# Attention before a top-1 mixture of experts: router logits issued one round later, their transposes two

## The chip, the cores and the metric

The kernel runs on one core of a Trainium2 chip. The time is the device time of one execution in microseconds (us), as the median of several runs. A profile is one further execution with the hardware profiler on. The engines: TensorE (PE, with its weight loads as PEld), VectorE (DVE), ScalarE (ACT), GpSimd (POOL); SyncE (SP) issues most DMAs. Each engine works through its own queue of instructions in the order in which the program wrote them, and waits on semaphores for the others.

## What is computed

The reference, cut to what matters:

```python
def _attn_ref(q, k, v, n_global, n_local):            # 4 x 8 heads, 768 rows, 64 wide; 8 and 96
    scores = np.matmul(q, k.transpose(0, 1, 3, 2)) / np.sqrt(D)
    keep = is_global | is_local                        # first 8 keys, and the last 96 up to the row's own
    scores = np.where(keep, scores + bias[None], -1e9)
    a = np.exp(scores - scores.max(-1, keepdims=True))
    a = a / (a.sum(-1, keepdims=True) + 1e-9)
    return np.matmul(a, v)

def _moe_ref(x, w_gate, w1, w2, capacity):             # x: 3072 x 512, 8 experts, capacity 80
    logits = x @ w_gate
    expert_idx = np.argmax(logits, axis=1)
    probs = np.exp(logits - logits.max(-1, keepdims=True))
    gate_w = (probs / (probs.sum(-1, keepdims=True) + 1e-9))[np.arange(N), expert_idx]
    for e in range(8):                                 # the 80 rows with the largest gate_w of expert e
        out[tok_idx] = gate_w[tok_idx, None] * (np.maximum(x[tok_idx] @ w1[e], 0) @ w2[e])
```

Attention's output `x`, 3072 rows of 512, goes into the router; each expert keeps the 80 of its rows with the largest gate.

## The kernel before

Attention works on 24 tiles `t` of 128 rows, each in two halves (`g` = 0 and 1, half of the heads each), so in 48 rounds `u` = 2t + g. The loop over `u` in `fast_path` writes the instructions of one round, and all engines' queues keep that order:

- `scores(u)`: the score matmuls (L181) into the three PSUM banks `ring`; for each of four head pairs DVE adds the bias table and takes the extreme in one step (`ts`, `nm`, L201), and ACT takes the exponential and its sum (`pwz`, `z`, L205). Amid them stand the transposes of round u-2 on PE (L242, L250, and L255 for finished rows), and for round u-1 the reciprocal of the sums (`invert`, DVE, L213 and L214) and the normalisation (`norm`, POOL, L222).
- `logits2`, in rounds with u%4==1: two PE transposes (L330) of the logits of two tiles, `lps<-ls`, and two DVE reductions into `lg` (L359).
- `copied(u-2)`: the transposed probabilities go from PSUM to `ta`, one half by ACT (L259), the other by DVE (L265).
- `logits1`, in rounds with u%4==0: four matmuls (L318; eight passes in the trace) of a finished pair of tiles `ut` with the router weights into the PSUM tile `lps`, and a DVE copy `ls<-lps` (L322). The pair of tiles t, t+1 comes at u = 2t+8, its `logits2` at 2t+9.
- `weigh(u-3)`: probabilities times values (L289, L298) into `pair`; once both halves of a tile are there, in even rounds, ACT copies `pair` out to `ut`, for the last tiles into parts of `kt` (L312).
- `routes(n)`: the next n steps of the routing of groups of tiles. The 24 tiles are routed in groups of 6, 6, 6, 4 and 2 (`GROUPS`). A group's steps are generators that wait in one list: maximum, difference, exponential and sum (`Route.all`, L505 to L511; the exponential is ACT's, L508), for the first group a scale (`Route.scale`), then `Route.rest`: the one-hot choice `oh` (L555), three compares `cf` against a row of thresholds (L545), two idle steps, the count of rows above each threshold (six matmuls on PE, L601, into another part of `lps`), its subtraction from `capm` (L536), two steps on `re` (L561, L562), the gate (L570, L571) and eight column operations on POOL (L581 to L588). A group's list is entered when `logits2` of its last tiles has been written. Up to round 40 a round takes 2 steps (3 with u%4==3), from round 41 on 5.

After round 46 the string `DRAIN` writes the last round's rest by hand: `r` is one step of `routes`, `a1` and `a2` are the two logits steps of tiles 20 and 21, `b1`, `b2`, `c1` to `c3` those of tiles 22 and 23 (`one`, L497 to L499), `n47` the last `invert` and `norm`, `w44` to `w47` the last `weigh`. Then come the search for each expert's threshold, the choice of its rows, and the experts.

All tiles in PSUM are tracked as wholes: an instruction that writes `lps` waits for earlier readers of `lps`, whatever columns they read.

Of the kernel before, what the change touches and what calls it, by code (L numbers as in the profile page):

```python
# [24 lines left out]
NT = B * NB  # L25
# [26 lines left out]
HELD, EVERY, AHEAD, LATE = 2, 3, 14, 2  # L52
FROM, INSIDE = 18, 14
HOLD = 20


DRAIN = (
# [14 lines left out]
def fast_path(tc, a, out, cst, x_dram, inp):  # L72
# [4 lines left out]
    with ExitStack() as ctx:  # L77
# [63 lines left out]
        with tc.tile_pool(name="at_sb", bufs=2) as sp, ExitStack() as sctx:  # L141
# [8 lines left out]
            def idle(n):  # L150
                wake = cst["svx"].rearrange("p s t -> p (s t)")
                for _ in range(n):
                    T.matmul(lps[:, :480], wake[:, :P], wake, start=True, stop=True, skip_group_check=True)

            def begin(u):
                st[u] = [
                    sp.tile([P, 4], F32, tag="nm", bufs=3, name=f"nm{u}"), sp.tile([P, 4], F32, tag="z", bufs=3, name=f"z{u}"),
                    sp.tile([P, 4, WH], F32, tag="ts", name=f"ts{u}"), pwz[u % 3][:, :4 * WH].rearrange("p (j k) -> p j k", j=4),
                ]
# [102 lines left out]
            def copied(u):  # L262
                spot = u - FROM
                ta, tp, n = st[u, "ta"]
                (A.copy if u == nu - 2 else V.tensor_copy)(out=ta[:, 1, :n], in_=tp[:, :n])  # L265
                if 0 <= spot < 2 * INSIDE:
                    r = TURN[spot // 2] * P
                    nc.sync.dma_start(
                        out=x_dram[r:r + P, :].rearrange("p (i g c) -> p i g c", i=2, g=2)[:, :, spot % 2], in_=ta[:, :, n - P:n])
                st[u, "ta"] = ta  # L270
# [45 lines left out]
            def logits1(t, n):  # L316
                for pr in range(NP):
                    T.matmul(  # L318
                        lps[32 * pr:32 * pr + 32, :n * P], cst["wgn"][:, pr, :], st[t, "ut"][:, pr, :n, :], start=True, stop=True,
                        skip_group_check=True)  # L320
                ls = sp.tile([P, n * P], F32, tag=f"ls{n}", name=f"ls{t}")
                (A.copy if t == NT - 2 else V.tensor_copy)(out=ls, in_=lps[:, :n * P])  # L322
                st[t, "l"] = ls

            def logits2(t, n):

                ls = st.pop((t, "l"))
                if n == 2:
                    for i in range(2):
                        T.transpose(out=part(t + i), in_=ls[:, P * i:P * i + P], identity=ident)  # L330
                else:
                    T.matmul(lgs(t), ls, cst["pick"], start=True, stop=True, skip_group_check=True)
                for i in range(n):
                    collect(t + i)

            def part(t):
                return lps[:, :P] if t % 2 else lps[:, 2 * P:3 * P]

            def lgs(t):
                if t == NT - 1:  # L340

                    if t not in st:
                        st[t] = psa.tile([P, 512], F32, tag="tp0", name="lgl")[:, :E]
                    return st[t]
                if t not in st:
                    st[t] = psa.tile([P, 512], F32, tag="tp1", name="lgk")[:, :E]
                return st[t]

            def collect(t):
                g = next(i for i in range(len(GROUPS)) if t < sum(GROUPS[:i + 1]))  # L350
                n, t0 = GROUPS[g], sum(GROUPS[:g])
                if t == t0:
                    st["rt"] = Route(nc, sp, cst, t0, n)
                rt = st["rt"]
                if n < 3:
                    rt.one(lgs(t), t - t0)
                else:
                    lp = part(t).rearrange("p (q k) -> p k q", q=NP)
                    V.tensor_reduce(out=rt.lg[:, t - t0, :], in_=lp[:, :E, :], axis=AX.X, op=ALU.add)  # L359
                    if t == t0 + n - 1:  # L360
                        routing.append(rt.all())
                        if t0 == 0:
                            routing.append(rt.scale(lps[:, P * NP - 1:]))
                if t == t0 + n - 1:
                    if t < NT - 1:
                        routing.append(rt.rest(lps[:, 3 * P:3 * P + E], cst["capm"]))
# [9 lines left out]
            def routes(n):  # L376
                for _ in range(n):
                    while routing and next(routing[0], END) is END:
                        routing.pop(0)

            routing, cst["later"], cst["landed"] = [], [], []
            nu = 2 * NT
            late = late_constants(nc, a, cst)
            keys = inp.keys(3)
# [6 lines left out]
            for u in range(nu - 1):  # L391
                if u == 0:
                    for _ in cst["first"]:
                        pass
                begin(u)
                scores(u)
                if u % 4 == 1 and 9 <= u:
                    logits2((u - 9) // 2, 2)
                if 2 <= u:
                    copied(u - 2)  # L400
                if u == 1:
                    for _ in window:
                        pass
                    for z in pwz:
                        G.memset(z[:, 4 * WH:], 0.0)
                    G.memset(cst["zero"], 0.0)
                if u > 2:
                    for _ in range(3):
                        next(late, None)
                if u % 4 == 0 and 8 <= u:  # L410
                    logits1((u - 8) // 2, 2)
                if 3 <= u:
                    idle(2 if u == 3 else 0)
                    weigh(u - 3)
                if u % 2 == 0 and 3 <= u // 2 + 2 < NT:
                    inp.load_q(u // 2 + 2, hold=u < HOLD)
                    for _ in range(1 + (u == 20)):
                        next(keys, None)
                if u % 2:
                    if 2 <= u // 2 + 1 < NT:  # L420
                        inp.load_v(u // 2 + 1, hold=u < HOLD)
                    for k in ASKS[u // 2]:
                        next(dict(w=ahead, o=wipe).get(k, iter(())), None)
                routes(5 if u > 40 else 2 + (u % 4 == 3))
            u = nu - 1
            begin(u)
            scores(u)
# [964 lines left out]
def build(tc, a, out):  # L1392
    nc = tc.nc
    with tc.tile_pool(name="cst", bufs=1) as cp, tc.tile_pool(name="dr", bufs=1, space=DRAM) as dp:
        x_dram = dp.tile([B * S, DM], F32, name="x_dram")
        lg_dram = dp.tile([B, P, NB, E], F32, name="lg_dram")
        sg_dram = dp.tile([E, P, NT], F32, name="sg_dram")
        cst = Constants(nc, cp)
        late_tiles(cst)
        with tc.tile_pool(name="at_in", bufs=1) as ip:  # L1400
            early = tc.manual_schedule(engines=ORDERED)
            early.__enter__()
            inp = Inputs(nc, a, ip)

            for n, t in (("rel", inp.vb[0]), ("bias", inp.vb[3])):
                cst[n], cst[n + "w"] = t[:, :2 * WH].rearrange("p (h k) -> p h k", h=2), t
            for i, n in enumerate(("r0", "k0", "b0")):
                cst[n] = inp.kt[1].rearrange("p q k -> p (q k)")[:, P * i:P * i + (NG if n == "k0" else P)]
            constants(nc, a, cst)
            inp.more(cst)  # L1410
            early.__exit__(None, None, None)
            fast_path(tc, a, out, cst, x_dram, inp)
            sure = nc.values_load(cst["sure"], min_val=0, max_val=1)
            with tc.If(sure < 1):
                general_path(tc, a, out, cst, x_dram, lg_dram, sg_dram)
# [44 lines left out]
```

## Time and profile before

| | us |
|---|---|
| median of 3 runs | 257.93 (257.54 to 258.23) |
| the profiled execution | 259.51 |
| its span, first to last instruction | 257.7 |
| attention's last exponentials end, about | 134 |
| PE, DVE, ACT, POOL busy | 239.6, 213.7, 208.0, 107.5 |

In the rows below, a busy time of an engine is a sum over a stretch of the span; in rows of the timeline the first number is the start in us from the span's start, the second the duration in us, and square brackets hold the idle time of that engine just before, with what ended it. Durations of neighbours on one engine can overlap a little, so the step from one start to the next is the better price of an instruction in a row.

### The profile page before, as it was taken

To read this page: it belongs to the slowest core of one execution; us is meant where nothing else is said; L and a number is where in the kernel's file an instruction comes from. 1 tells how busy PE (TensorE), PEld (TensorE's weight loads), DVE (VectorE), ACT (ScalarE), POOL (GpSimd) and SP (SyncE) were. 2 spreads that over 40 slices of the span, in tenths; PEclk is the share of its full clock that TensorE was granted. 3 is DMA by queue.
4 is the path that set the end of the run, shared out by engine and by line. 5 is a ranking of instruction groups with operands and counts; after the bars stand their busy time and mean duration, and the time that the engine had idled before them with its cause. 6 is when DMAs were issued, how large, how long until landed. Compare 5 with 4: busy or idle time off the path is not lost.

```text
span 257.7 us, 9711 instructions
## 1 busy us (share of the span) xinstructions
PE 239.6 (93%) x3587; PEld 169.2 (66%) x3587; DVE 213.7 (83%) x782; ACT 208.0 (81%) x584; POOL 107.5 (42%) x214
## 2 busy tenths in 40 slices
PE   7989998998899999999998798999999999999991
PEld 2567766766677777877667655666666666666660
DVE  3777778987779799898987778999999898999860
ACT  3889899998899999999886636887979898979740
POOL 7667674644445745457470638810000022221111
PEclk9999999999999999999999659999999999999998
DMA  5758999999998999988649976999999999999101
GB/s 145 235 159 218 330 287 280 282 304 300 274 301 247 287 284 316 319 251 230 216 138 311 384 265 204 347 333 401 404 410 408 407 397 398 389 405 364 51 25 36
DMA packets 49086, 73.06 MB, mean 284 GB/s; under 512 B 3688, under 2 KB 23528, under 8 KB 49032
## 3 DMA queue, kind: packets, MB, share of 16 engines
q1 hardware_dynamic: 47864, 69.74, 81.3%
q0 software_dynamic: 1024, 2.62, 3.2%
q8 instruction: 30, 0.49, 0.8%
q14 instruction: 24, 0.20, 0.3%
q10 hardware_dynamic: 144, 0.00, 0.0%
HBM read 58.46 MB, written 13.89 MB: 281 GB/s over the span
## 4 chain that ended last, share of the span: by engine, by line
PE 63%; ACT 13%; DVE 10%; DMA 4%; issue 4%; POOL 3%; SPq 0%; POOLq 0%; DVEq 0%; ACTq 0%
PE hp L843 17%; PE yp L843 17%; ACT pwz L205 9%; PE ring L181 6%; PE pair L289 5%; PE pair L298 3%; DMA kt<-in_kT_dram 3%; PE tp L242 3%; ACT ta L259 2%; DVE ts L201 2%; POOL pwz L222 2%; PE tp L898 2%; PE lps L318 1%; DMA q<-in_q_dram 1%; PE lps L330 1%
## 5 line engine op out<-in xcount | busy, mean ns | idle before, releaser
L205 ACT ACTIVATE pwz<-ts,nm 128x168 f32<-128x168 f32 (+1 forms) x192 | 81.5, 427 | 10.3 <-DVE z L213 6.0
L222 POOL TENSOR_TENSOR pwz<-pwz,z 128x672 f32<-128x672 f32 (+2 forms) x48 | 60.2, 1255 | 53.4 <-DVE z L214 35.5
L201 DVE CUSTOM_DVE_ANT_0 ts<-ring,tab 128x168 f32<-128x168 f32 (+1 forms) x192 | 53.2, 315 | 11.7 <-PE ring L181 11.0
L181 PE MATMUL ring<-kt,q 64*64 64x64 f32 (+3 forms) x1088 | 41.0, 275 | 1.0 <-DMA q<-in_q_dram 0.5
L926 POOL DMA_INDIRECT out_dram<-vb,si x8 | 10.0, 1248 | 76.3 <-ACT xt5h L836 37.9
L205 ACT ACTIVATION_READ_ACCUMULATOR pwz<-ts,nm 128x1 f32 x192 | 36.5, 190 | 0.0
L181 PEld LDWEIGHTS ring<-kt,q 64*64 64x64 f32 x1088 | 32.5, 137 | 4.7 <-issue 2.2
L289 PE MATMUL pair<-ta,va 104*64 104x128 f32 (+1 forms) x368 | 30.5, 285 | 5.1 <-ACT ut L312 3.5
L289 PEld LDWEIGHTS pair<-ta,va 104*64 104x64 f32 (+1 forms) x368 | 19.3, 136 | 14.1 <-issue 7.1
L265 DVE COPY ta<-tp 128x512 f32<-128x512 f32 (+2 forms) x46 | 28.3, 616 | 0.0
L259 ACT COPY ta<-tp 128x512 f32<-128x512 f32 (+2 forms) x47 | 23.8, 507 | 0.5 <-ACT pwz L205 0.5
L242 PE MATMUL tp<-ident,pwz 64*128 64x64 f32 x376 | 21.7, 235 | 1.4 <-POOL pwz L222 0.5
L242 PEld LDWEIGHTS tp<-ident,pwz 64*128 64x128 f32 x376 | 15.3, 138 | 9.1 <-POOL pwz L222 3.5
L817 DVE TENSOR_TENSOR w_3l<-w,w_3h 128x1024 fp32r<-128x1024 f32 x16 | 19.6, 1223 | 1.4 <-ACT w_3h L813 1.3
L817 DVE TENSOR_TENSOR w_0l<-w,w_0h 128x1024 fp32r<-128x1024 f32 x15 | 18.3, 1222 | 2.0 <-ACT w_0h L813 2.0
L298 PE MATMUL pair<-ta,vb 64*64 64x64 f32 x640 | 18.7, 231 | 0.0
L817 DVE TENSOR_TENSOR w_1l<-w,w_1h 128x1024 fp32r<-128x1024 f32 x15 | 18.3, 1220 | 0.0
L817 DVE TENSOR_TENSOR w_2l<-w,w_2h 128x1024 fp32r<-128x1024 f32 x15 | 18.3, 1218 | 0.0
L298 PEld LDWEIGHTS pair<-ta,vb 64*64 64x64 f32 x640 | 13.2, 133 | 6.8 <-issue 6.7
L813 ACT CAST w_3h<-w 128x1024 fp32r<-128x1024 f32 x16 | 16.7, 1045 | 0.3 <-PE yp L843 0.3
L813 ACT CAST w_2h<-w 128x1024 fp32r<-128x1024 f32 x15 | 15.9, 1058 | 1.2 <-PE hp L843 1.0
L201 DVE DVE_READ_ACCUMULATOR2_ANT nm<- 128x1 f32 x192 | 16.0, 83 | 0.0
(441 smaller groups left out, 525.9 us busy)
## 6 DMA issues: line engine op xcount, KB each, us to landing
w<-in_w_dram SPq DMA_DIRECT2D x64, 512.0 KB
kt<-in_kT_dram SPq DMA_DIRECT2D x23, 272.0 KB
out_dram<-zero SPq DMA_DIRECT2D x12, 512.0 KB
q<-in_q_dram SPq DMA_DIRECT2D x23, 256.0 KB
vb<-in_vb_dram SPq DMA_DIRECT2D x20, 256.0 KB
va<-in_va_dram SPq DMA_DIRECT2D x20, 208.0 KB
x_dram<-ta SPq DMA_DIRECT2D x28, 128.0 KB
x_dram<-kt SPq DMA_DIRECT2D x6, 256.0 KB
```

The lines of the kernel that those rows point to most:

```text
L181: T.matmul(sc[hh][64 * i:64 * i + 64, pp, o:o + e - c], q[h, pr * P + 64 * i:pr * P + 64 * i + 64], kt[h, pr, c0 + c:c0 + e], start=True, ...
L201: V.tensor_tensor_reduce(out=ts[:, j, :w], in0=sc[hh][:, pp, :w], in1=tab, scale=-0.125, scalar=3.0e38, op0=ALU.add, op1=ALU.min, accum_ou ...
L205: A.activation(out=pw[:, j, :w], in_=ts[:, j, :w], func=AF.Exp, bias=nm[:, j:j + 1], scale=-1.0, accum_out=z[:, j:j + 1],)
L222: eng.tensor_tensor(out=p, in0=p, in1=zs.unsqueeze(2).broadcast_to(list(p.shape)), op=ALU.mult)
L242: T.transpose(out=tps[i][:, 64 * j:64 * j + 64], in_=pw[hs[i], o:o + P], identity=ident[hs[i], hs[i]])
L259: A.copy(out=ta[:, 0, :n], in_=tps[0][:, :n])
L265: (A.copy if u == nu - 2 else V.tensor_copy)(out=ta[:, 1, :n], in_=tp[:, :n])
L289: T.matmul(up[pp][64 * hh:64 * hh + 64], va[:n, 64 * h:64 * h + 64], ta[:n, :, 64 * j:64 * j + 64], start=g == 0 if t < NT - 1 else pp == ...
L298: T.matmul(up[pp][h, 64 * i:64 * i + 64], vb[k, i, 2 * g + pp, :], ta[k, i, 256 + 64 * pp:320 + 64 * pp], start=False, stop=True, skip_gro ...
L813: A.copy(out=hi, in_=src)
L817: V.tensor_tensor(out=lo, in0=src, in1=hi, op=ALU.subtract)
L843: T.matmul(ps, p, q, start=first and i == 0, stop=last and i == 2, skip_group_check=True)
```

## The change

The rounds of `logits1` and `logits2` come from two tables. For tiles t below 16 (`SOON`) `logits1` is at u = 2t+9, a round with u%4==1, and `logits2` at 2t+11, with u%4==3. For t = 16 and 18 they stay at 2t+8 and 2t+9 (rounds 40, 41 and 44, 45). The third routing step of a round goes from u%4==3 to u%4==0. `DRAIN` is unchanged.

```diff
+SOON = 16
             routing, cst["later"], cst["landed"] = [], [], []
+            first = {2 * t + (9 if t < SOON else 8): t for t in range(0, NT - 4, 2)}
+            second = {2 * t + (11 if t < SOON else 9): t for t in range(0, NT - 4, 2)}
...
                 scores(u)
-                if u % 4 == 1 and 9 <= u:
-                    logits2((u - 9) // 2, 2)
+                if u in second:
+                    logits2(second[u], 2)
...
-                if u % 4 == 0 and 8 <= u:
-                    logits1((u - 8) // 2, 2)
+                if u in first:
+                    logits1(first[u], 2)
                 if 3 <= u:
                     idle(2 if u == 3 else 0)
                     weigh(u - 3)
...
-                routes(5 if u > 40 else 2 + (u % 4 == 3))
+                routes(5 if u > 40 else 2 + (u % 4 == 0))
```

The line numbers of the changed kernel are one higher up to `routes` (L182 for L181, L323 for L322) and three higher behind it (L604 for L601, L548 for L545). The first two groups enter the routing list two rounds later (19 and 31 instead of 17 and 29), the third and later ones in the same round as before, behind what is still in the list.

The first place is the end of round 40 on PE, before: the logits of tiles 16 and 17, `weigh(37)`, and the scores of round 41.

```order
L318 MATMUL lps<-ut_2449,wgn 32x256 x4
L289 MATMUL pair<-ta_2689,va 64x128 x4
L298 MATMUL pair<-ta_2689,vb_118 64x64 x8
L181 MATMUL ring_207<-kt_114,q_109 64x104
L181 MATMUL ring_207<-kt_114,q_109 64x64
```

The same place after; the count's pair of rows comes six times, and the scores of round 41 follow.

```order
L319 MATMUL lps<-ut_2445,wgn 32x256 x4
L290 MATMUL pair<-ta_2678,va 64x128 x4
L299 MATMUL pair<-ta_2678,vb_118 64x64 x8
L604 LDWEIGHTS cf_2587
L604 MATMUL lps<-oh,cf_2587 127x8
```

On DVE, that round's copies and small steps after the change:

```order
L266 COPY ta_2744<-tp_38_2743 128x512
L323 COPY ls_2773<-lps 128x256
L539 TENSOR_TENSOR capm<-capm,lps 127x8
L564 TENSOR_SCALAR re<-oh 128x48
L202 ISA ts_2800,nm_2798<-ring_207,tab 128x168
```

The count of the second group came at the end of round 38; now it stands in round 40, behind that round's copy `ls` by its wait on `lps`, and its subtraction (L539) follows the copy on DVE.

The second place is the end of round 45 on DVE, before, from the reductions of the logits of tiles 18 and 19 to the first score step of round 46.

```order
L359 TENSOR_REDUCE lg_3131<-lps 128x8 x2
L265 COPY ta_3104<-tp_43_3103 128x512
L536 TENSOR_TENSOR capm<-capm,lps 127x8
L561 TENSOR_SCALAR re<-oh 128x48
L562 TENSOR_TENSOR re<-re,sx_2302 128x48
L570 TENSOR_SCALAR sx_2302<-sx_2302 128x6
L201 ISA ts_3164,nm_3162<-ring_208,tab_160 128x128
```

The same place after, again from the reductions to the first score step.

```order
L360 TENSOR_REDUCE lg_3129<-lps 128x8 x2
L266 COPY ta_3102<-tp_43_3101 128x512
L548 TENSOR_TENSOR cf_3076<-sx_2427,kval_65 128x254 x2
L202 ISA ts_3160,nm_3158<-ring_208,tab_160 128x128
L202 ISA nm_3158 128x1
```

Two of the third group's three compares now stand behind the copy `ta`. On PE the count that reads them stays at the end of round 45, ahead of the scores of round 46, in both kernels. The steps L536 to L570 moved into round 46.

The third place is the end of attention. On POOL before, from the last normalisation but one (round 46) to the steps of the fourth group:

```order
L585 CAST bx<-og 128x6x8
L92 MEMSET w_2_0_3270 1x1
L92 MEMSET w_2_1_3281 1x1
L586 TENSOR_TENSOR bx<-oh,pval 128x6x8
L587 TENSOR_TENSOR bx<-og,bx 128x6x8
L588 COPY bx<-oh 128x6x8
L222 TENSOR_TENSOR pwz_202<-pwz_202,z_3225 128x128
L506 TENSOR_TENSOR ex_3129<-mx_3132,lg_3131 128x32
```

And after:

```order
L223 TENSOR_TENSOR pwz_202<-pwz_202,z_3221 128x128
L588 CAST bx<-og 128x6x8
L589 TENSOR_TENSOR bx<-oh,pval 128x6x8
L590 TENSOR_TENSOR bx<-og,bx 128x6x8
L591 COPY bx<-oh 128x6x8
L509 TENSOR_TENSOR ex_3127<-mx_3130,lg_3129 128x32
```

The four column operations of the third group moved from ahead of the last normalisation to behind it, ahead of the fourth group's difference `ex`. On DVE there, before:

```order
L555 TENSOR_TENSOR oh<-eq_3130,m_3134 128x32
L545 TENSOR_TENSOR cf_3364<-tail,kval_65 128x254 x2
L497 TENSOR_REDUCE mx_3377<-lgk 128x1
L498 SCALAR_TENSOR_TENSOR eq_3376<-lgk,mx_3377,pref 128x8
L545 TENSOR_TENSOR cf_3392<-tail,kval_65 128x127
```

And after:

```order
L558 TENSOR_TENSOR oh<-eq_3128,m_3132 128x32
L500 TENSOR_REDUCE mx_3375<-lgk 128x1
L501 SCALAR_TENSOR_TENSOR eq_3374<-lgk,mx_3375,pref 128x8
L548 TENSOR_TENSOR cf_3364<-tail,kval_65 128x254 x2
L548 TENSOR_TENSOR cf_3388<-tail,kval_65 128x127
```

The fourth group's two compares moved from ahead of the steps on the logits of tile 22 (`lgk`) to behind them.

## Rows read from the trace of the kernel before

**Rows 1.** The page: busy time, share and instructions of PE; PE's clock in tenths, 40 slices.

```profile
PE 239.6 (93%) x3587; PEld 169.2 (66%) x3587; DVE 213.7 (83%) x782; ACT 208.0 (81%) x584; POOL 107.5 (42%) x214
PEclk9999999999999999999999659999999999999998
```

**Rows 2.** Stretches: length, busy us (instructions) of PE, PEld, DVE, ACT, POOL; clock, DMA.

```profile
80.36:99.05 18.69, 17.82 (x452) 13.82 (x447) 16.20 (x91) 17.97 (x69) 10.90 (x15) 1.00 0.93 279
99.05:117.06 18.01, 18.01 (x462) 14.25 (x463) 16.01 (x90) 17.25 (x66) 10.00 (x13) 1.00 0.93 292
```

**Rows 3.** Chain that ended last: start us, us, what.

```profile
54.22 7.79 DMA kt<-in_kT_dram
...
76.14 0.45 PE lps L601 x6
...
81.34 0.47 ACT ta L259
...
97.22 0.47 ACT ta L259
...
99.05 0.66 PE pair L289 x8
...
115.35 0.59 PE pair L289 x8
```

**Rows 4.** Grouped instructions: line, engine, operation, count | busy, mean ns | idle before, releaser.

```profile
L289 PE MATMUL pair<-ta,va 104*64 104x128 f32 (+1 forms) x368 | 30.5, 285 | 5.1 <-ACT ut L312 3.5 <-issue 1.2 <-ACT kt L312 0.4
L330 PE MATMUL lps<-ident,ls 128*128 128x128 f32 x22 | 4.8, 301 | 0.2 <-DVE ls L322 0.2
```

**Rows 5.** Timeline, PE and DVE, end of round 40.

```profile
113.20 0.46 PE L298 MATMUL pair<-ta,vb 64*64 64x64 f32 x16
113.49 0.86 PE L181 MATMUL ring<-kt,q 64*64 64x104 f32 x24
113.69 0.41 DVE L322 COPY ls<-lps 128x256 f32<-128x256 f32 x1
...
114.38 0.33 DVE L201 CUSTOM_DVE_ANT_0 ts<-ring,tab 128x168 f32<-128x168 f32 x1 [0.18 <-PE ring L181]
```

**Rows 6.** Timeline, DVE and ACT, end of round 43.

```profile
122.32 0.23 ACT L508 ACTIVATE ex<-ex 128x48 f32<-128x48 f32 x1
122.59 0.20 DVE L511 TENSOR_REDUCE sx<-ex 128x6 f32<-128x48 f32 x1 [0.53 <-ACT ex L508]
...
123.25 0.43 ACT L205 ACTIVATE pwz<-ts,nm 128x168 f32<-128x168 f32 x1 [0.70 <-DVE z L213]
```

**Rows 7.** Timeline, DVE and PE, end of round 45.

```profile
127.51 0.68 DVE L265 COPY ta<-tp 128x512 f32<-128x512 f32 x1
127.65 0.46 PE L601 MATMUL lps<-oh,cf 128*127 128x8 bf16 x6 [0.52 <-DVE lg L359]
...
128.04 0.67 PE L181 MATMUL ring<-kt,q 64*64 64x128 f32 x16
128.15 0.16 DVE L536 TENSOR_TENSOR capm<-capm,lps 127x8 f32<-127x8 f32 x1
...
128.76 0.28 DVE L201 CUSTOM_DVE_ANT_0 ts<-ring,tab 128x128 f32<-128x128 f32 x1
```

**Rows 8.** Timeline, POOL and DVE, end of attention.

```profile
132.99 0.21 POOL L585 CAST bx<-og 128x48 bf16<-128x48 f32 x1
...
133.69 0.21 POOL L588 COPY bx<-oh 128x48 bf16<-128x48 bf16 x1
134.47 0.68 POOL L222 TENSOR_TENSOR pwz<-pwz,z 128x128 f32<-128x128 f32 x1 [0.57 <-DVE z L214]
135.40 0.25 POOL L506 TENSOR_TENSOR ex<-mx,lg 128x32 f32<-128x32 f32 x1 [0.24 <-DVE mx L505]
...
136.50 0.76 DVE L545 TENSOR_TENSOR cf<-tail,kval 128x254 bf16<-128x254 f32 x2
...
138.45 0.29 DVE L545 TENSOR_TENSOR cf<-tail,kval 128x127 bf16<-128x127 f32 x1 [0.42 <-ACT ex L499]
```

## Prediction

> **What bounds the kernel now.** I read the page's first lines for the whole, the chain of waits for which engine sets the pace where, the grouped instructions for the waits that the change aims at, and then, in order of time, the places where the order of the instructions changes. TensorE (PE) is the busiest engine, and its clock is at full level in all of the attention; it falls only behind it, in the slices around 145 us [rows 1]. But PE's share is no verdict on a stage. In attention (48 rounds, some 2.6 us each) the chain alternates: up to 62.01 it runs into a transfer of keys that lands then, whatever the engines had done before it [rows 3]. From 80.36 to 99.05 ScalarE (ACT) sets the pace: it is busy 17.97 of 18.69 us, PE 17.82 [rows 2], and its copies `ta` start at 81.34 and, six rounds later, 97.22: 2.65 us a round [rows 3]. From 99.05 to 117.06 it is PE, busy in all of 18.01 us [rows 2]; the first matmuls of `weigh` start at 99.05 and, six rounds later, at 115.35: 2.72 a round [rows 3]. After that ACT leads until 122.3, and then VectorE (DVE), which has the most small routing work there [rows 6, 7]. At the end of attention the last two tiles' routing runs through all engines, one step after the other [rows 8].
>
> What the change can win is in the grouped rows: the first matmuls of `weigh` wait 3.5 us in all for ACT's copy `ut` [rows 4], which empties the sums in every even round so that `weigh` can begin new ones a round later. With u%4==1 the logits' transposes stand between the two, with u%4==3 nothing does. Now the transposes (4.8 us for 22, so 0.44 for a pair [rows 4]) come to stand there, in time that PE lost anyway; eight pairs of tiles move, so eight times 0.44, or 3.5 us, is the most that this can cover. PE's load per round also becomes more even.
>
> **The change part by part.** No operation is added or removed; only places in the queues change, and through them the waits.
>
> *Rounds up to 62 us.* Four of the eight pairs come by 62 us, worth 1.8 at most. But the keys that landed at 62.01 took 7.79 us on the way [rows 3], and the chain stood still for them; only as far as their issue comes earlier is a gain kept. I take -0.2, bounds -0.9 (half of it) and 0.
>
> *Rounds 22 to 28.* The count of the first group of tiles (0.45 us on PE, at 76.14 [rows 3], in a stretch that PE leads) goes two rounds later, where ACT leads. At most -0.45; in its new place it can cost 0.1. I take -0.2.
>
> *Rounds 29 to 39.* Under ACT nothing is to be had. In the stretch that PE leads the floor is ACT's 2.65 against 2.72: 6 x 0.07 = 0.4 us, and the second group's count leaves it too. I take -0.3, bounds -0.45 and 0.
>
> *Round 40.* Here two parts of the change meet. Tile 16 keeps its round, so its logits and their copy `ls` out of `lps` stand in round 40; the second group, two rounds late, brings its count into the same round. The count writes `lps` too, and as the program tracks a whole tile, it waits for the copy. In the trace the last `weigh` matmuls of that round start at 113.20, the scores of the next one at 113.49; the copy runs from 113.69 to 114.10 [rows 5]. The count (0.39 us from its start to the scores behind it, 127.65 to 128.04 [rows 7]) would end at 114.49, and the scores start 1.0 us later. The first DVE step on them had already waited 0.18 for PE at 114.38 [rows 5], so DVE has no cover there; for ACT, whose exponentials follow, I take 0.1 off. So +0.9; bounds 0 (ACT leads again two rounds later and has had work enough) and 1.0.
>
> The Trainium skill ("PSUM — Partial Sum Buffer", section "PSUM bank collisions raise a hardware error") says that accesses by two engines to one bank must be kept apart even where their columns differ. By that rule this wait is no accident of bookkeeping. The trace agrees as far as it goes: the third group's count waits 0.52 us for the DVE reductions of other columns of the same tile [rows 7]. If the count could run beside the copy, the sum would come out 0.6 lower.
>
> *Rounds 42 to 44.* Before, DVE's sum of the exponentials stands in round 43 and waits 0.53 us for ACT's exponential, which comes behind all of that round's; ACT then waits 0.70 for DVE [rows 6]. After, the sum stands a round later, and the exponential is long there. ACT could go on at 122.55 instead of 123.25. The steps that leave round 43 load DVE in round 44 instead (copy, maximum, sum, compare). I take -0.55, bounds -0.7 and 0.
>
> *Round 45.* The third group's three compares `cf` stood ahead of the DVE copy `ta` of round 45; now the last two stand behind it, and PE's count waits for them, with the scores of round 46 queued behind the count. The copy starts at 127.51, the next DVE step at 128.15 [rows 7]; two compares of the same kind take 0.76 [rows 8]. With the 0.55 gained above they end at 127.51 + 0.64 + 0.76 - 0.55 = 128.36; with 0.39 for the count the scores start at 128.75 instead of 128.04. DVE's first step on them started 0.72 behind them, at 128.76 [rows 7], and now would at 129.45. That is 0.7 later, though the round began 0.55 earlier: +1.25, bounds 0.3 (DVE's four small steps leave this round, 128.15 to 128.76, and cover it) and 1.35.
>
> *Round 46.* Those four steps and a reciprocal now stand ahead of the last DVE scores, 0.6 us more. ACT copies `kt` before its next exponential, which I take to hide nearly all of it (no row bears on it but that both lie on ACT). I take +0.05, bounds -0.1 and 0.5.
>
> *The last steps.* On GpSimd (POOL) four column operations, from 132.99 to 133.90, stood before the last normalisation, which waited 0.57 for DVE anyway (134.47); now they stand behind it and ahead of the fourth group's difference `ex`, at 135.40, which had only 0.24 of slack [rows 8]. It would start at 135.15 + 0.91 = 136.06, 0.66 later; ACT's exponential of it follows, and the copies of the last tiles' logits stand behind that on ACT. On DVE the group's two compares (0.76), done at 136.50 before, now stand behind the steps on the last logits and ahead of the compare at 138.45, which had 0.42 of idle time before it [rows 8]. The two delays lie on one path: the first brings some 0.5, the second some 0.35 over the idle time. I take +0.6 for both; bounds 0.2 and 0.85. What follows (search, choice, the experts) has the same instructions.
>
> Sum: -0.2 - 0.2 - 0.3 + 0.9 - 0.55 + 1.25 + 0.05 + 0.6 = +1.55 us. The profiled execution took 259.51 with a span of 257.7, so a profile of after would show a span of some 259.25; the timed runs had a median of 257.93, and the forecast is 259.5.
>
> **The rivals.** A, faster: the spread pays in all rounds. For it: PE's waits for `ut` are real [rows 4], and PE leads much of the chain. Say that five of the eight pairs are hidden in those waits (5 x 0.44 = 2.2) and that the transfer at 62 us takes 1.0 of it back: -1.2. Rounds 22 to 39 give 0.5 and round 44 gives 0.55 as above; round 40 costs 0.1, round 45 its lower bound of 0.3, the last steps 0.6 and round 46 0.05. Together -1.2, or 256.7. The case decides once the rounds before 40 keep over 2.25 us, which is what my later terms make together (2.8 - 0.55), or less if those come at their lower ends. Against it: the stop at 62.01 [rows 3], and ACT's 96% in the rounds behind it [rows 2].
>
> B, no difference: the count of round 40 is hidden, as ACT has work in store, and the last steps cost their lower bound: 1.55 - 0.8 - 0.4 = +0.35, 258.3. For it: with three score banks the engines run some half a round apart. Against it: DVE waits for PE at just that place.
>
> C, slower by the clock: the later count and the waits in the last rounds leave PE thinner used. The clock went to 1.2 GHz in the slices behind attention, where PE waits on the routing [rows 1]; if the fall came some 4 us earlier, the matmuls of the last steps would take up to twice as long: some 2 us more, 261.5. Against it: the clock stood at 2.4 GHz through all of attention [rows 1], with the wait of 0.52 us in it [rows 7].
>
> That the change might not do what it says is no rival: the order of the instructions shows all eight pairs moved.
>
> **How the numbers follow.** Under 0.3% (0.77 us) a measurement of this kernel can't tell a difference from none. My sum has the chance 0.55, A 0.21, B 0.17, C 0.07. Of my own sum a little falls within 0.3%, of B nearly all, of C none: slower 0.58, same 0.21, faster 0.21. The range: downward it goes to A's middle (256.7); upward my sum with round 40, round 45 and the last steps at their ends, +0.1, +0.1 and +0.25, and the early gains at zero, +0.7: 260.65, cut to 260.6, since these don't come together. That leaves some 0.1 on either side.
>
> **What would show it.** In the trace of after: the copy `ls`, the count and then the scores one behind the other in round 40, with a wait of some 0.6 us at the count; no wait of DVE for the exponential `ex` of the third group; the count in round 45 ended by the compares `cf`; POOL's `ex` of the fourth group behind four column operations; two compares between the steps on the last logits. The waits of `weigh` for `ut` should shrink in u%4==3, and the start of round 23 should still sit on the keys. The forecast is wrong if attention is ahead by over 1 us at round 36, or if the engines' distance hides the wait of round 40.

## The result, and the profile after

The changed kernel is slower: 260.5 us in the median of 16 runs, against 258.24 for 16 runs of the kernel before beside it; the ratio is 1.0091, with a 95% interval of 1.0066 to 1.0117, so 1.7 to 3.0 us and 2.35 in the middle. In later runs it was 1.0111 (1.0072 to 1.0150). The forecast was 259.5, or +1.55 on the median it started from: right in sign and in the mechanism up to the search, short by some 0.8 us in size. The median lies just inside the stated range (256.7 to 260.6), and that is in part luck: the upper end was put together from the sum's own terms at their ends, while what came on top stood in none of them (below), and six later runs of the changed kernel had a median of 260.76.

The page of after: the span, PE's busy time and PE's clock in 40 slices, to be read beside [rows 1].

```profile
span 258.5 us, 9711 instructions
PE 241.2 (93%) x3587; PEld 170.8 (66%) x3587; DVE 213.3 (83%) x782; ACT 207.1 (80%) x584; POOL 103.9 (40%) x214
PEclk9999999999999999999997559999999999999997
```

The span grew by only 0.8 us here, less than the time. That is chance: the profiled execution of before had a stop in rounds 20 to 22 that other executions of the same order do not have (below). So spans of single executions can't be subtracted; the rounds can. The table does that. A round is the time from one reciprocal `z` on DVE (L214, after: L215) to the next; most rounds agree within 0.03 us from one execution to another, and where an execution has a stop, that of a later run with the same order up to there stands in (for before mostly `e6_drain_late_only`, the same until round 46, for after `c_after_again`). One choice matters: rounds 25 and 26 took 2.70 and 2.73 us in the profile of before, with no wait for a transfer in them, and 2.45 and 2.55 in the later run, which the table takes. With the first pair, rounds 22 to 28 would differ by -0.5, and the sum would be some +1.2.

| stretch | forecast | before | after | difference |
|---|---|---|---|---|
| rounds 8 to 21 | -0.2 | 35.96 | 35.79 | -0.15 |
| rounds 22 to 28 | -0.2 | 18.04 | 17.98 | -0.05 |
| rounds 29 to 39 | -0.3 | 29.29 | 28.83 | -0.45 |
| rounds 40 and 41 | +0.9 | 5.24 | 6.31 | +1.05 |
| rounds 42 to 44 | -0.55 | 8.98 | 8.43 | -0.55 |
| round 45 | +1.25 | 2.69 | 3.77 | +1.1 |
| rounds 46 and 47 | +0.05 | 4.95 | 5.11 | +0.15 |
| last `z` to the first matmul `jb` | +0.6 | 6.29 | 6.83 | +0.55 |
| sum up to `jb` | +1.55 | | | +1.6 |
| `jb` to the end | 0 | 117.29 | 118.94 | +1.65 |

The sum of the forecast up to the search is what the table shows, within that choice. What it didn't have is the last line; of that, on average over runs, some 0.8 us count (below).

The waits at which the change aims, in the grouped rows (as [rows 4]), with the count beside them:

```profile
L290 PE MATMUL pair<-ta,va 104*64 104x128 f32 (+1 forms) x368 | 30.3, 285 | 2.2 <-ACT ut L313 1.5 <-ACT kt L313 0.4
L331 PE MATMUL lps<-ident,ls 128*128 128x128 f32 x22 | 4.8, 301 | 0.0
L604 PE MATMUL lps<-oh,cf 128*127 128x8 bf16 x24 | 2.5, 198 | 1.6 <-DVE cf L548 0.7 <-DVE ls L323 0.4 <-DVE lg L360 0.2
```

`weigh` waits 1.5 us for `ut` instead of 3.5, so the change reached its aim; and of these 2.0 us the rounds up to 39 give back some 0.7 by the table. In exchange the count waits 1.6 us where it waited 0.8. The places where it does, in the timeline. Round 40, PE and DVE (as [rows 5]):

```profile
110.54 0.41 DVE L323 COPY ls<-lps 128x256 f32<-128x256 f32 x1
111.00 0.46 PE L604 MATMUL lps<-oh,cf 128*127 128x8 bf16 x6 [0.40 <-DVE ls L323]
111.39 0.86 PE L182 MATMUL ring<-kt,q 64*64 64x104 f32 x24
...
112.29 0.33 DVE L202 CUSTOM_DVE_ANT_0 ts<-ring,tab 128x168 f32<-128x168 f32 x1 [0.53 <-PE ring L182]
```

The copy, the count and the next scores stand one behind the other, and DVE then waits 0.53 for those scores. Rounds 42 to 43, DVE and ACT (as [rows 6]):

```profile
119.77 0.23 DVE L509 TENSOR_TENSOR ex<-mx,lg 128x48 f32<-128x48 f32 x1
...
120.31 0.23 ACT L511 ACTIVATE ex<-ex 128x48 f32<-128x48 f32 x1
120.46 0.43 ACT L206 ACTIVATE pwz<-ts,nm 128x168 f32<-128x168 f32 x1
```

ACT goes on at once behind the exponential `ex`, where it had waited 0.70 for DVE; the round takes 2.59, before 3.18. Round 45, DVE and PE (as [rows 7]):

```profile
124.88 0.68 DVE L266 COPY ta<-tp 128x512 f32<-128x512 f32 x1
125.01 0.22 PE L604 MATMUL lps<-oh,cf 128*127 128x8 bf16 x2 [0.20 <-DVE lg L360]
125.47 0.75 DVE L548 TENSOR_TENSOR cf<-sx,kval 128x254 bf16<-128x254 f32 x2
125.94 0.61 PE L604 MATMUL lps<-oh,cf 128*127 128x8 bf16 x4 [0.71 <-DVE cf L548]
126.49 0.67 PE L182 MATMUL ring<-kt,q 64*64 64x128 f32 x16
...
127.21 0.29 DVE L202 CUSTOM_DVE_ANT_0 ts<-ring,tab 128x128 f32<-128x128 f32 x1 [0.98 <-PE ring L182]
```

Two of the count's six matmuls can start, four wait for the compares behind `ta`; the scores of round 46 wait behind them on PE, and DVE, which had been the late engine here, stands 0.98 us. The end of attention, POOL, ACT and DVE (as [rows 8]):

```profile
133.08 0.68 POOL L223 TENSOR_TENSOR pwz<-pwz,z 128x128 f32<-128x128 f32 x1 [0.41 <-DVE z L215]
133.71 0.22 POOL L588 CAST bx<-og 128x48 bf16<-128x48 f32 x1
...
134.34 0.22 POOL L591 COPY bx<-oh 128x48 bf16<-128x48 bf16 x1
134.52 0.23 POOL L509 TENSOR_TENSOR ex<-mx,lg 128x32 f32<-128x32 f32 x1
...
136.55 0.95 DVE L548 TENSOR_TENSOR cf<-tail,kval 128x254 bf16<-128x254 f32 x3
```

From the end of the last normalisation (133.76) to `ex` it is 0.76 us instead of 0.25, and the three compares stand in a row.

### The profile page after: what moved, and what is told of

Its sections match the earlier page's. It is cut to its first block, busy times and chain, and to the rows that moved or that the text cites. A ratio compares the mean times of both kernels' runs of the same rounds, so it can differ in the third digit from the quotient of the medians.

```text
span 258.5 us, 9711 instructions
## 1 busy us (share of the span) xinstructions
PE 241.2 (93%) x3587; PEld 170.8 (66%) x3587; DVE 213.3 (83%) x782; ACT 207.1 (80%) x584; POOL 103.9 (40%) x214
## 4 chain that ended last, share of the span: by engine, by line
PE 59%; ACT 16%; DVE 12%; POOL 6%; issue 4%; POOLq 0%; DMA 0%; DVEq 0%; ACTq 0%
PE yp L846 17%; PE hp L846 17%; ACT pwz L206 12%; PE ring L182 4%; PE pair L290 4%; ACT ta L260 3%; DVE ts L202 3%; POOL pwz L223 3%; PE pair L299 2%; PE tp L243 2%; PE lps L319 2%; PE tp L901 2%; PE lps L597 2%; DVE z L214 1%; DVE ta L266 1%
## 5 line engine op out<-in xcount | busy, mean ns | idle before, releaser
L206 ACT ACTIVATE pwz<-ts,nm 128x168 f32<-128x168 f32 (+1 forms) x192 | 81.4, 426 | 10.2 <-DVE z L214 5.8
L182 PE MATMUL ring<-kt,q 64*64 64x64 f32 (+3 forms) x1088 | 40.8, 270 | 1.3 <-DVE z L214 0.4
L182 PEld LDWEIGHTS ring<-kt,q 64*64 64x64 f32 x1088 | 32.5, 134 | 4.4 <-issue 1.7
```

What stands on the lines that cost most here:

```text
L182: T.matmul(sc[hh][64 * i:64 * i + 64, pp, o:o + e - c], q[h, pr * P + 64 * i:pr * P + 64 * i + 64], kt[h, pr, c0 + c:c0 + e], start=True, ...
L206: A.activation(out=pw[:, j, :w], in_=ts[:, j, :w], func=AF.Exp, bias=nm[:, j:j + 1], scale=-1.0, accum_out=z[:, j:j + 1],)
```

## The experiments

All are edits of a few characters in the call of `routes`, that is, in how many routing steps a round takes, unless the text says otherwise; each ratio is against the kernel before on the same chip.

**Two ways to bring the late order back, and one to make it alone.** The spread of the logits with the late routing as before:

```diff
-                routes(5 if u > 40 else 2 + (u % 4 == 0))
+                routes(5 if u > 40 else 2 + (u % 4 == 0) + (20 <= u < 24))
```

> The changed kernel with four extra routing steps (one more in each of rounds 20 to 23): the logits keep their new rounds, but from round 26 on the routing stands where it stood before the change (no count beside the copy `ls` in round 40, compares of the third group ahead of `ta`, column operations ahead of the last normalisation). Theory L (the slowdown is made by late routing steps: round 40 +0.9, rounds 42 to 46 +0.75, last steps +0.6): without them the early gain of some 0.7 us is left, so 0.3 to 1 us below the kernel before, about 257.5. Rival S (the moved logits themselves cost, the late steps are hidden): about as slow as the changed kernel, 260 to 260.5. Rival C (a different fall of TensorE's clock makes the difference): the time follows the mean granted clock, whatever the order.

259.14 us, ratio 1.0051 (1.0013 to 1.0088): between the expectations, 1.1 us slower than before instead of 0.5 faster. The rounds tell a part of it. Round 45 is 2.69 again and the last steps 6.3, as theory L has it, but the extra steps put three compares into one round, and round 24 takes 2.93 instead of 2.71 (after: 2.45), round 36 2.97 (after: 2.59). So this run isn't the clean spread it was meant to be; its rounds 8 to 47 take 105.56 us, 0.4 more than before's in the table, and what is left of its 1.1 us isn't explained.

A cleaner one, which moves only the pairs of tiles that do not end a group, with every routing step left in its round:

```diff
-SOON = 16
+SOON = (0, 2, 6, 8, 12, 14)
...
-            first = {2 * t + (9 if t < SOON else 8): t for t in range(0, NT - 4, 2)}
+            first = {2 * t + (9 if t in SOON else 8): t for t in range(0, NT - 4, 2)}
...
-                routes(5 if u > 40 else 2 + (u % 4 == 0))
+                routes(5 if u > 40 else 2 + (u % 4 == 3))
```

(`second` likewise.)

> The changed kernel with only those pairs of tiles moved that do not end a group (0, 2, 6, 8, 12, 14; pairs 4 and 10 keep their rounds), and the third routing step back at u%4==3: every routing step stands in the round in which it stood before the change, six of the eight pairs of logits are moved. Theory L (moving the logits helps a little, the late routing costs): 0 to 0.7 us under before, and in the trace rounds 12 and 32 (2.78 before) at 2.45 to 2.6. Rival S (moving the logits costs some 1 us, by stalls that come and go from run to run): 0.7 to 1.3 over before, as the run with the spread and four extra steps was.

258.45 us, ratio 1.0016 (0.9986 to 1.0047), so from 0.4 us under before to 1.2 over: no difference that can be told from noise. The time alone does not shut out rival S (0.7 to 1.3 over). The rounds speak against it: rounds 8 to 47 take 105.33 us here and 105.15 in the table for before. Moving the logits doesn't give any to speak of either. Rounds 12 and 32 went from 2.78 to 2.44 and 2.59, as expected, but round 13 went from 2.31 to 2.73 and round 40 from 2.59 to 2.87. `weigh` waits 2.3 us for `ut`, 1.2 less than before, and hardly any of this reaches the time.

The late order alone, in the kernel before:

```diff
-                routes(5 if u > 40 else 2 + (u % 4 == 3))
+                routes(5 if u > 40 else 2 + (u % 4 == 3) - (20 <= u < 24))
```

> The kernel before with four routing steps fewer (one less in each of rounds 20 to 23): the logits keep their old rounds, but late routing stands as in the changed kernel from round 35 on (the count in round 40, the compares behind `ta` in round 45, the column operations behind the last normalisation). Theory L: as slow as the changed kernel or more, 2.25 us over before and some more as the early gain is missing: 260 to 261. Rival S: as before, within 0.4 us. In the trace L expects round 40 about 1 us longer than its neighbours, and round 45 too.

260.17 us, ratio 1.0076 (1.0045 to 1.0107): as slow as the changed kernel within the intervals, with the logits where they were. Its round 45, DVE and PE:

```profile
124.39 0.68 DVE L265 COPY ta<-tp 128x512 f32<-128x512 f32 x1
124.53 0.22 PE L601 MATMUL lps<-oh,cf 128*127 128x8 bf16 x2 [0.20 <-DVE lg L359]
124.99 0.75 DVE L545 TENSOR_TENSOR cf<-sx,kval 128x254 bf16<-128x254 f32 x2
...
125.45 0.61 PE L601 MATMUL lps<-oh,cf 128*127 128x8 bf16 x4 [0.71 <-DVE cf L545]
126.00 0.67 PE L181 MATMUL ring<-kt,q 64*64 64x128 f32 x16
...
126.72 0.29 DVE L201 CUSTOM_DVE_ANT_0 ts<-ring,tab 128x128 f32<-128x128 f32 x1 [0.98 <-PE ring L181]
```

The same waits to 0.01 us, and the round takes 3.77. Round 40 it does not reproduce, though that was expected: with the third step of a round still at u%4==3, the count of the second group stands in round 39 here (at 107.59 us), ahead of the logits of tiles 16 and 17 and their copy `ls` (at 110.82), and not behind the copy. Rounds 39 and 40 take 2.95 and 2.87, together 0.65 over before. So this run shows that the late order is slow without the moved logits, but says nothing on the wait for `ls`.

**The terms one by one.** Round 40's count taken out of the changed kernel, the rest of the late order kept:

```diff
-                routes(5 if u > 40 else 2 + (u % 4 == 0))
+                routes(5 - 4 * (u == 41) if u > 40 else 2 + (u % 4 == 0) + (20 <= u < 24))
```

> The changed kernel with the second group's count out of round 40 (four extra steps in rounds 20 to 23, taken back in round 41, so that rounds 42 to 47 and the last steps are those of the changed kernel). Theory L: 0.9 us (0.6 to 1.1) below the changed kernel, with round 40 at 2.6 us in the trace. Rival S: no difference from the changed kernel.

261.33 us, ratio 1.0121 (1.0073 to 1.0169), from 6 runs: not faster than the changed kernel. Round 40 took 2.87, so the 0.8 were saved, but rounds 24 and 36 cost 0.5 and 0.4 by the three compares, and the profiled execution had stops in several other rounds. Once more:

> The kernel without the count in round 40 once more, since its first runs were few and its trace full of rounds lengthened at other places (rounds 23, 30, 33, 34, 38 and 46). Theory L, with what its trace showed: round 40 gives 0.8 back against the changed kernel, the three compares in one round take 0.5 in round 24 and 0.3 in round 36; so about the changed kernel's time, 260 to 260.8. Rival: it is really slower than the changed kernel, 261.3 again, and something in it is not understood.

260.67 us, ratio 1.0122 (1.0078 to 1.0165), beside 260.76 for the changed kernel in the same runs: in line with the sum -0.8 + 0.5 + 0.4, though six runs can't tell it from 1 us more or less. It shows the size of the count's part of round 40 in the trace, and that such steps can't be moved for nothing.

Round 40 kept, rounds 42 to 47 and the last steps as before:

```diff
+                routes(5 + 4 * (u == 41) if u > 40 else 2 + (u % 4 == 0))
```

> The changed kernel with four more routing steps in round 41: round 40 keeps its count beside the copy `ls`, rounds 42 to 47 and the last steps stand as before the change. Theory L: 1.35 us (1.0 to 1.7) below the changed kernel: 0.75 of rounds 42 to 46 and 0.6 of the last steps. Rival S: no difference from the changed kernel.

259.34 us, ratio 1.0047 (1.0015 to 1.0078), by the ratios 1.1 us below the changed kernel; expected were 1.35 (1.0 to 1.7). Round 40 takes 3.64. The stops of the profiled execution hide the rounds behind it.

The last steps alone, put back in the changed kernel and made late in the kernel before (the words behind # name the kernel that was edited):

```diff
+                routes(5 + 4 * (u == 46) if u > 40 else 2 + (u % 4 == 0))    # the changed kernel
+                routes(5 - 4 * (u == 46) if u > 40 else 2 + (u % 4 == 3))    # the kernel before
```

> The changed kernel with four more routing steps in round 46, so that only the last steps stand as before the change (POOL's column operations ahead of the last normalisation, the fourth group's compares ahead of the steps on the last logits); rounds 40 and 45 stay as changed. Theory L: in the trace the stretch from the last `z` reciprocal to the first matmul `jb` goes from 6.83 us back to 6.29. Theory K (the longer last steps also make TensorE's clock fall earlier or stay down longer): the time below the changed kernel by 0.6 to 1.5, of which 0.5 are the steps themselves, and more runs with a mean granted clock of 0.97 or above. Rival (the clock's fall has nothing to do with these steps): 0.5 us, the clock as in the changed kernel.

> The kernel before with four routing steps fewer in round 46, so that only the last steps stand as in the changed kernel; all rounds up to 46 are those of the kernel before. Theory L: 6.8 us from the last `z` reciprocal to `jb`, 0.5 us over before, 258.6. Theory K: 0.5 to 1.5 over before, with the clock lower in more runs. Rival: no difference, if something else was late there.

The first: 259.68 us, ratio 1.0086 (1.0043 to 1.0129), which can't be told from the changed kernel: the 0.5 us of theory L and the 0.6 to 1.5 of theory K don't show in the time, and the intervals are too wide to decide between them. The trace shows the step itself: from the last `z` to `jb` 6.28 us instead of 6.83. The end of attention there, POOL and DVE, reads as in [rows 8], with `ex` behind the normalisation at once:

```profile
134.51 0.68 POOL L223 TENSOR_TENSOR pwz<-pwz,z 128x128 f32<-128x128 f32 x1 [0.25 <-ACT ta L260]
...
135.43 0.25 POOL L509 TENSOR_TENSOR ex<-mx,lg 128x32 f32<-128x32 f32 x1 [0.24 <-DVE mx L508]
136.50 0.76 DVE L548 TENSOR_TENSOR cf<-tail,kval 128x254 bf16<-128x254 f32 x2
138.49 0.29 DVE L548 TENSOR_TENSOR cf<-tail,kval 128x127 bf16<-128x127 f32 x1 [0.42 <-ACT ex L502]
```

The second: 258.96 us, ratio 1.0047 (1.0013 to 1.0081), so 0.3 to 2.1 us over before, and 6.82 us from the last `z` to `jb`. The last steps cost 0.55 in both directions, and in the time possibly more.

**The other way round: routing earlier.** Three steps in every round from 25 on, so that the third group finds the list empty (again with the edited kernel's name behind #):

```diff
+                routes(5 if u > 40 else 2 + (u > 24 or u % 4 == 0))    # the changed kernel
+                routes(5 if u > 40 else 2 + (u > 24 or u % 4 == 3))    # the kernel before
```

> The changed kernel with three routing steps in every round from 25 to 40: the second group's routing is done before round 41, so the third group starts there at once, with its count in round 43, and no count meets a copy `ls`. Theory L: the late rounds cost 1 us less than before the change (rounds 43 and 44 were 3.2 us each, now 2.7), the spread's gain stays: 256.7 to 257.6, faster than before. Rival S (moving the logits costs by itself, some 1 us, as the mean of the run with the spread alone may say): 258 to 259.

> The kernel before with three routing steps in every round from 25 to 40: the same early routing of the second and third group, the logits in their old rounds. Theory L: 0.5 to 1 us under before, 257.2 to 257.7, and 0.3 to 0.7 over the same routing with the logits moved. Rival S: under the one with the logits moved by some 1 us.

Both expectations of theory L were missed: 260.49 (ratio 1.0104, 1.0064 to 1.0143) and 259.61 (1.0064, 1.0029 to 1.0098), both slower than before. In the second, rounds 43 and 44 take 3.88 and 3.97 instead of 3.2. Round 43, which has the count, shows the same pattern:

```profile
120.42 0.69 DVE L265 COPY ta<-tp 128x512 f32<-128x512 f32 x1
...
121.02 0.50 DVE L545 TENSOR_TENSOR cf<-sx,kval 128x254 bf16<-128x254 f32 x1
121.58 0.28 PE L601 MATMUL lps<-oh,cf 128*127 128x8 bf16 x2 [0.70 <-DVE cf L545]
...
123.02 0.33 DVE L201 CUSTOM_DVE_ANT_0 ts<-ring,tab 128x168 f32<-128x168 f32 x1 [0.96 <-PE ring L181]
```

Again a compare behind `ta`, the count behind the compare, the scores behind the count, and 0.96 us of waiting on DVE. Not all of it is the order: the granted clock falls to 1.2 GHz at 122.1, amid those scores, and comes back at 125.5, so that in round 44 PE is busy throughout (the stretch: length, busy us of PE, PEld, DVE, ACT, POOL; the third number from the right is the granted clock):

```profile
123.47:127.44 3.97, 3.97 (x84) 2.74 (x80) 3.03 (x16) 2.89 (x11) 1.58 (x2) 0.74 0.50 154
```

With five steps in a round, the two idle steps of `rest` no longer put a round between the compares and the count. I had only counted the DVE steps, and not looked for this. On rival S it says nothing, as the two runs' intervals overlap.

**The clock.** The changed kernel again, and with six matmuls of zero use in the last steps:

> The changed kernel itself, on the chip of these runs, for the ratio on the same chip and a second trace of it. All theories: 2 to 2.6 us over before. Theory L expects rounds 40 and 45 at 3.65 and 3.77 again, and 6.8 us from the last `z` reciprocal to `jb`.

260.76 us, ratio 1.0111 (1.0072 to 1.0150). Rounds 40 and 45 take 3.64 and 3.77, the last steps 6.82, and from `jb` to the end 118.85 us. So the line below the sum in the table came twice; both of these executions had a mean granted clock of 0.960.

```diff
+            wake = cst["svx"].rearrange("p s t -> p (s t)")
+
+            def fill(n):
+                for _ in range(n):
+                    T.matmul(ring[1][:, :480], wake[:, :P], wake, start=True, stop=True, skip_group_check=True)
+
+            fill(3)
             go(choice, 99)
             cn = lps[:, 3 * P + 2 * E:3 * P + 3 * E]
             count(nc, cn, [rt])
+            fill(3)
```

> The changed kernel with six matmuls of zero use (480 columns each, into a score bank that is free by then) on TensorE in the last steps, three ahead of the last count and three behind it, where PE waits for DVE. Theory K (about 0.9 us of the slowdown is TensorE's clock, down longer since PE waits longer in the last steps): the clock's time at 1.2 GHz, which was 17.6 us in the mean of the changed kernel's runs and 14.4 before, goes back by some 3 us, and the time goes down by 0.5 to 1 us, to 259.6 to 260.1. Rival (the clock only goes along with slow runs, it doesn't make them; or it falls because of what comes after `jb`): no change of the clock's share, time the same or up to 0.5 higher, as the fill stands in PE's queue.

260.29 us, ratio 1.0080 (1.0048 to 1.0112). The clock followed: over its 12 runs the time at 1.2 GHz (twice one minus the mean granted clock, times the span) is 12.8 us in the mean, after 17.6 (16 runs, and 19.3 in the six later ones) for the changed kernel and 14.4 (86 runs) for the kernel before. By the ratios the time went down by 0.3 us against the changed kernel's first runs and by 0.8 against its later ones, no more than these intervals can tell from nothing. The fill itself cost 0.35 us: 7.18 from the last `z` to `jb` instead of 6.83.

## Why the prediction was right, point by point

**What bounds what.** Two engines take turns in leading, and where ACT leads, PE's waits cost nothing: of 2.0 us of waits that went away, the rounds up to 39 kept some 0.7. Rival A rested on those waits being on the path, and fell with the result and with the clean spread (1.0016).

**The keys at 62 us.** This step was wrong, though its value (-0.2) held. I read the transfer that landed at 62.01 as a fixed mark that takes gains back. It was an accident of that execution: rounds 20 to 22 of before took 2.86, 3.31 and 3.62, those of a run with the same order 2.66, 2.65 and 2.59, and the changed kernel's 2.65, 2.77 and 2.60. Nothing was taken back; there was little to take, because round 13 paid most of what round 12 gained (2.78 to 2.44, and 2.31 to 2.6). Such stops stand in 11 of the 14 profiles, in other rounds each time.

**Rounds 22 to 39.** -0.2 and -0.3 were forecast, -0.05 and -0.45 came: the right total by the table (some 0.4 more with the profile's own rounds 25 and 26), from rounds 32 (2.78 to 2.59) and 36 (2.88 to 2.59) most of all.

**Round 40.** +0.9 forecast, +1.05 measured with round 41, just over the upper bound. The chain of copy, count and scores is there as the prediction put it, and is worth 0.8: round 40 takes 3.64, and 2.85 to 2.87 in the runs with the moved logits and the count elsewhere. The other 0.3 comes with the moved logits (2.59 to 2.87 in the clean spread), for which the prediction had no term here. The Trainium skill's "PSUM — Partial Sum Buffer" (section "PSUM bank collisions raise a hardware error") wants accesses of two engines to one bank kept apart even where the columns differ. The trace agrees as far as it goes: the count waits 0.40 us for a copy of other columns of `lps`. The rows don't show whether it is the bank or the tracking of the whole tile that demands it; a count into another bank wasn't tried.

**Rounds 42 to 47.** -0.55 came to the digit. Round 45's +1.25 came as +1.1, with the releasers as foreseen; the scores start 0.27 us behind the end of the compares, where 0.39 was taken, as the first matmuls of the count run ahead. Rounds 46 and 47 cost 0.15 instead of 0.05.

**The last steps.** +0.6 forecast, +0.55 in the traces of after and of the kernel before with only these steps late. Rival B, which had this and round 40 hidden, fell.

**What the sum left out.** "What follows has the same instructions" was taken as no change. In the profiled execution the part from `jb` on took 1.65 us more, 1.3 of it in the first 16 us. PE's clock shows where. The stretches of before and after (length, busy us of PE, PEld, DVE, ACT, POOL; the third number from the right is the granted clock), first of before:

```profile
138.00:140.00 2.00, 1.69 (x19) 1.56 (x18) 1.43 (x10) 1.24 (x6) 0.00 (x0) 1.00 0.79 245
140.00:142.00 2.00, 1.22 (x27) 0.98 (x26) 1.79 (x8) 1.12 (x2) 0.00 (x0) 1.00 1.04 400
142.00:144.00 2.00, 1.88 (x47) 1.80 (x48) 1.48 (x7) 0.95 (x2) 0.97 (x5) 0.85 1.04 397
...
154.00:158.00 4.00, 3.27 (x17) 1.95 (x16) 3.33 (x5) 1.62 (x4) 3.39 (x3) 1.00 0.41 96
```

And of after:

```profile
138.00:140.00 2.00, 1.00 (x12) 0.70 (x13) 1.47 (x10) 1.19 (x4) 0.00 (x0) 0.77 1.01 390
140.00:142.00 2.00, 1.94 (x48) 1.76 (x44) 1.87 (x7) 1.01 (x1) 0.00 (x0) 0.50 1.05 405
142.00:144.00 2.00, 2.00 (x30) 1.68 (x29) 1.23 (x4) 1.11 (x2) 1.62 (x8) 0.50 0.97 361
...
153.00:158.00 5.00, 4.43 (x17) 2.64 (x16) 3.17 (x5) 1.13 (x3) 3.95 (x4) 0.69 0.40 127
```

After, PE is busy for 1.00 of 2.00 us from 138 to 140, where it waits for the compares and the steps behind them, and the clock goes to 1.2 GHz there, some 4 us earlier than before; it comes back some 2.5 us later. That is rival C, which I had put beside my sum, at 0.07, instead of into it.

This pair of executions overstates it. In the four other profiles with the late last steps and no fill, the part from `jb` on takes 117.5 to 117.9 us, at mean granted clocks of 0.970 to 0.973; in the seven with the last steps of before it takes 117.3 to 118.5; and in the clean spread's the clock falls at `jb` as well. Over all runs the time at 1.2 GHz was 17.6 us in the mean against 14.4, and within the runs of one kernel a run takes some 0.25 us more for each of these us (0.24 for before, 0.27 for the changed kernel): 3.2 x 0.25 = 0.8 us, about what was missing. With the late last steps alone it was 16.1 us, against 13.9 for before on the same chip; with only the last steps put back, 16.3. That work for PE in these waits keeps the clock up is shown by the fill, which brought it to 12.8 us. That the clock makes the 0.8 us is not: 4.8 us of clock should have brought 1.2 us by that slope, less 0.35 for the fill; 0.3 or 0.8 came, by which of the changed kernel's runs one takes, and the intervals reach from nothing to all of it.

The clock also falls inside attention, which neither the prediction nor the table has. In three of the seven profiles with the new round 45 (the late order alone, the first run without the count in round 40, and the fill) it goes to 1.2 GHz within 1 us of that round's end. Round 46 takes 3.28 and 3.38 us in the first two, where the profile of after has 2.66, and round 47 takes 2.80 in the third instead of 2.45. Round 46 of the late order alone, with PE busy throughout:

```profile
127.14:130.42 3.28, 3.28 (x56) 2.50 (x54) 2.65 (x17) 2.63 (x11) 1.31 (x1) 0.50 0.37 115
```

In the four profiles with the rounds 42 to 46 of before and no stop there (before, the two spreads, the late last steps alone) it stays at 2.4 GHz until attention ends. How much of the missing 0.8 us is the clock, here or behind attention, and how much stops, stays open.

## What to carry to other kernels

A wait on an engine that doesn't lead is no store of time: count what it is worth in the stretch where another engine leads before moving work into it. When a producer is issued later, follow its last consumer to the end of the program and look for what then shares a round: here three instructions in a row across two queues (a copy or compare on DVE, a count on PE, the next scores on PE) cost 0.8 us in round 40 and 1.1 in round 45, more than what had moved takes itself (the count 0.4, two compares 0.75), and moving the routing earlier ran into the same pattern. And compare round by round, not span by span: most rounds here repeat to 0.03 us, while whole runs of the kernel before reach from 257.2 to 259.7 us, with stops that fall into other rounds each time and a clock that differs from run to run.

## What the runs showed of the hardware that I had not expected

The stops: single rounds of attention lengthened by 0.4 to 2.6 us in 11 of 14 profiles, with transfers of keys or values named at a few of them (`kt` at 62.01 in the profile of before, [rows 3]), and not in the next execution of the same order. And the clock's time at 1.2 GHz between attention and the experts, which was 10.2, 13.7 or 17.1 us in the profiled executions, differs from run to run of one kernel as well: the mean granted clock of the changed kernel's runs went from 0.960 to 0.972. In six of the 14 profiles the clock fell inside attention too.
